# First block of a two-layer linear-attention kernel: values first, weight folding in pieces, one written order on all engines

## The chip, the core and the metric

The program runs on one core of one Trainium2 chip. A core has five engines with a queue each: TensorE (PE; matrix products, with PEld for its loads of the stationary operand), VectorE (DVE), ScalarE (ACT), GpSimd (POOL) and SyncE (SP, which here only issues DMA transfers). They run side by side and wait for each other by semaphores. The metric is device time in microseconds of one execution, lower is better. The median of three runs before the change is 1398.45 us (1397.73 to 1398.7).

## The reference

Two layers, each an attention part and a dense part, on x of 2048 rows by 640, all float32:

```
x = x + A(layernorm(x));  x = x + B(layernorm(x));  and both once more
A: q, k, v = x @ wqkv, 32 heads of 20
   pq = q @ w_phi[h], pk = k @ w_phi[h]
   phi = [softmax(p), softmax(-p)]            (40 features a head)
   o = phi_q (phi_k^T v) / (phi_q (phi_k^T 1) + 1e-6);  A = o @ wo
B: mish(x @ w1 + b1) @ w2, inner width 1536
```

The sums over all 2048 rows in phi_k^T v stand between the making of the features and their use, so A has a first pass over all rows (features of q and k, values, the sums) and a second one (averages, product with wo, residual).

## The kernel before, in words

Rows are taken in 8 blocks of 256, a block as two tiles of 128. Every float32 product with a weight is made of three faster ones: operand and weight are split into a high part (rounded by ACT, a copy) and a low part (DVE or POOL subtracts the high part from the original), and hi by hi, hi by lo and lo by hi are summed. A tile of 128 rows by 640 columns takes 2 halves of 320 columns x 5 chunks of the contraction x 3 = 30 products (`project`, `project_half`, line 344).

Since w_phi is linear, it is folded into the weights of q and k once, at the start: `fold_phi` (line 237) multiplies the transposed raw weights with a block-diagonal matrix `bd` of w_phi, piece by piece (5 chunks x 2 groups of columns). A product of it appears as two records of PE. A piece has three such products; ACT copies its high part out of PSUM and DVE makes the low part.

A block of x is normalised (`norm_stats` on DVE, `norm_scale` on POOL and DVE, `normed` on ACT), transposed on PE in three steps (`Transposed.step`, 4, 4 and 2 transposes, line 280) and split into hi and lo there (ACT copy line 116, DVE subtract line 286).

`attend_first` is the first pass. For each block and each tile it makes "k", "q" and "v" in an order given in a tuple; block 0 has v0, q0, v1, k0, q1, k1. Each of them is a Python generator: its products and the copy of the result out of PSUM come first, and each later step of the list advances the pending ones by one stage (row maxima and minima with the subtractions; exp on ACT; sums, reciprocal on DVE and the scaling on POOL; for q the transpose on DVE, line 425, and four transfers to DRAM, line 429; for k the sums over rows on PE, line 416).

PSUM holds two wide tiles ("mm", for the result of a project) and four narrow ones ("one", for folding, transposes and the sums). A q result goes to one of two buffers (`query_tile`), which is free again when the four transfers of the q tile two before it have landed. `v_tile` has two buffers, `row_tile` ("xn") four, `big_tile` five, `x_tile` two.

What sets the order: the whole is traced in one block that a planner orders, engine by engine, by a model of the times. Within `tc.manual_schedule(engines=...)` the instructions of the engines named keep the order in which they were written; other instructions can still be placed between them. Before the change only SP is written by hand at the start: transfers of `bd` and the raw q weights, of block 0 of x, the rest of them, then the value weights `wv`, then the raw k weights. `tc.issue_after(ins)` keeps what is traced on that instruction's engine behind it; `act()` uses it to chain ACT's instructions. Folding of the q weights stands before the first products, folding of the k weights before k0.

Of the kernel before, what the change touches and what calls it, by code (L numbers as in the profile page):

```python
# [8 lines left out]
F32 = mybir.dt.float32  # L9
# [7 lines left out]
P = 128  # L17
S = 2048
D = 640
# [23 lines left out]
def kernel(  # L43
# [63 lines left out]

    last_act = [None]

    def act(*args, **kw):  # L110

        if last_act[0] is None:
            ins = nc.scalar.activation(*args, **kw)
        else:
            with tc.issue_after(last_act[0]):
                ins = nc.scalar.activation(*args, **kw)
        last_act[0] = ins.ins
# [4 lines left out]

    def split(hi, lo, src, stage):

        st = stage()[:, :D]
        nc.sync.dma_start(st, src)
        nc.scalar.activation(hi, st, AF.Copy)
        nc.vector.tensor_tensor(lo, st, hi.bitcast(F32), op=ALU.subtract)
# [37 lines left out]

    def load_v_weights():

        ws = [r1_pair(k) for k in range(KD)]
        for k in range(KD):  # L170
            split(ws[k][0][:, D:2 * D], ws[k][1][:, D:2 * D], wv[k * P:(k + 1) * P, :],
                  (row_tile, row_tile, v_tile, v_tile, big_tile)[k])
        return ws

# [52 lines left out]
    def fold_phi(ws, bd, raw):  # L227

        pss = {}
        for k, c in ((0, 0), (1, 0), (2, 0), (3, 0), (0, 1), (1, 1), (2, 1), (3, 1), (4, 0), (4, 1)):  # L230
            if c == 0:
                mm = None if k % 2 else mm_tile()
                pss[k] = [one_tile(), one_tile()] if k % 2 else [mm[:, 0], mm[:, 1]]
            ps = pss[k][c]
            for t in range(3 * c, 3 * c + 3):
                r, rows = raw[t]
                nc.tensor.matmul(ps[:, (t % 3) * 120:(t % 3) * 120 + rows],
                                 r[:rows, k * P:(k + 1) * P], bd[:rows, t, :rows],
                                 start=True, stop=True)
            n0, n1 = (0, 360) if c == 0 else (360, D)  # L240
            hi, lo = ws[k][0][:, n0:n1], ws[k][1][:, n0:n1]
            nc.scalar.activation(hi, ps[:, :n1 - n0], AF.Copy)
            nc.vector.tensor_tensor(lo, ps[:, :n1 - n0], hi.bitcast(F32), op=ALU.subtract)

# [83 lines left out]

    def project(xts, t, ws, col, ps=None):

        if ps is None:
            mm = mm_tile()
            ps = [mm[:, 0], mm[:, 1], mm]
        for c in range(2):
            project_half(ps[c], xts, t, ws, col, c)
        return ps
# [10 lines left out]
    def both(ps):  # L347

        return ps[2][:, :, :HC]


    def query_tile(i):
        return r2_wide(10 + i % 2, F32).rearrange("p s d -> p (s d)")

    def features(ps, e, pool_sub):
# [11 lines left out]
        for s, op in ((0, ALU.max), (1, ALU.min)):  # L367
            nc.vector.tensor_reduce(m[:, s], eh[:, 1], axis=AX.X, op=op)
        (nc.gpsimd if pool_sub else nc.vector).tensor_tensor(
            eh[:, 0], eh[:, 1], m[:, 0].unsqueeze(2).to_broadcast([P, H, DH]), op=ALU.subtract)  # L370
        nc.vector.tensor_tensor(eh[:, 1], m[:, 1].unsqueeze(2).to_broadcast([P, H, DH]), eh[:, 1],
                                op=ALU.subtract)
        yield
# [13 lines left out]
    def attend_first(layer, x_src, first):  # L387


        def fetch_normed(b):  # L390
            if layer:
                return load_turned(n2_d[b], [row_tile] * 3)
            xt = fetch(x_src, b)
            norm_scale(b, [norm_stats(t, xt) for t in range(BT)])
            return xt
# [24 lines left out]

        def queries(xts, i, ps=None):
            e = query_tile(i)
            yield from features(project(xts, i % BT, q_ws, 0) if ps is None else ps, e, True)

# [7 lines left out]

        def values(xts, i, v):
            vv = v.rearrange("p (h d) -> p h d", d=DH + 1)
            act(vv[:, :, DH], ident[:, :H], AF.Copy, scale=0.0, bias=1.0)
            if i < BT:
                pv = project(xts, i, kv_ws, D, [one_tile(), one_tile()])
                for c in range(2):
                    act(vv[:, c * H // 2:(c + 1) * H // 2, :DH],
                        pv[c][:, :HC].rearrange("p (h d) -> p h d", d=DH), AF.Copy)  # L440
            else:
                pv = project(xts, i % BT, kv_ws, D)
                act(vv[:, :, :DH].rearrange("p (c h) d -> p c h d", c=2),
                    both(pv).rearrange("p c (h d) -> p c h d", d=DH), AF.Copy)
            yield

        if first is None:
            with tc.manual_schedule(engines={mybir.EngineType.SP}):
                bd = big_tile()[:120, :720].rearrange("p (t c) -> p t c", t=6)
                nc.sync.dma_start(bd[:, :3], phi_bd[:, :3])  # L450
                raw = load_raw(0, range(3))
                xt = fetch_normed(0)
                nc.sync.dma_start(bd[:, 3:], phi_bd[:, 3:])
                raw += load_raw(0, range(3, 6))
                nxt = normed(0, xt).all()
                q_ws = [r2_pair(k) for k in range(KD)]
                fold_phi(q_ws, bd, raw)
                kv_ws = load_v_weights()
                raw = load_raw(1)
            nc.sync.dma_start(mask, head_mask)  # L460
        else:
            nxt, kv_ws = first
            q_ws = load_q_weights()
        for b in range(NB):
            xts = nxt
            order = ("k0", "k1", "v0", "v1", "q0", "q1")
            if b == 0:
                order = ("v0", "q0", "v1", "k0", "q1", "k1")
            elif b == 1:
                order = ("k0", "q0", "k1", "v0", "q1", "v1")  # L470
            elif b == NB - 1:
                order = ("k0", "k1", "v0", "v1", "q0")
            vs = [v_tile() for _ in range(BT)]
            for n, (kind, t) in enumerate(order):
# [5 lines left out]
                if b == 0 and n == 3:  # L480
                    if layer == 0:
                        fold_phi(kv_ws, bd, raw)
                    kva, kvz = one_tile(), one_tile()
                if b == NB - 1 and n == 3:
                    loaded = {0: load(0)}
                if b + 1 < NB:
                    if n == 0:
                        xt = fetch_normed(b + 1)
                    elif n == 2:
# [3 lines left out]
                g = {"k": lambda: keys(xts, i, vs[t]), "q": lambda: queries(xts, i),  # L493
                     "v": lambda: values(xts, i, vs[t])}[kind]()
                next(g)
                advance()
                pending.append(g)
            if b == 1:
                if layer == 0:
                    spill_qk_weights(kv_ws, q_ws)  # L500
                o_ws = load_o_weights()

        def rest():
# [8 lines left out]
            project_half(ps[1], xts, 1, q_ws, 0, 1, range(3, KD))  # L512
            pending.append(queries(xts, NT - 1, ps))
            next(pending[-1])
# [166 lines left out]
    def dense(x_src, x_dst, w1s, w2s, first, last):  # L681
# [97 lines left out]
        for i in range(len(steps) + SKEW):  # L779
# [26 lines left out]
            if i == len(steps) - 1 and not last:  # L806
                with tc.issue_after(exps[0]):
                    kv_ws = load_v_weights()
            if i >= SKEW:
# [89 lines left out]
```

## Time and profile before

| what | value |
|---|---|
| median of three runs | 1398.45 us |
| the profiled execution's own time | 1396.09 us |
| its span, first to last instruction | 1394.3 us |
| PE busy | 1380.7 us (99%) |
| DVE, ACT, POOL busy | 1075.5, 583.3, 440.0 us |
| DMA, q1, share of 16 engines | 44.2% |
| granted TensorE clock, mean | 0.999 |

The profiled execution is 2.36 us below the median of the runs, and its span 1.79 us below its own time. In a timeline a row gives start, duration, engine, line and operation, `x4` that four instructions in a row are merged into it (it then ends with the last one's end), and in brackets the engine's idle time before it with what ended it. Products overlap in PE's pipe, so the cost of one is the distance between two starts and not its duration. In the rows `mm<-big,raw` and `one<-big,raw` are folding, `one<-ident,xn` transposes, and products with `r1` use the value and k weights, those with `r2` the q weights.

### The profile page before, as it was taken

To read this page: it belongs to the slowest core of one execution; us is meant where nothing else is said; L and a number is where in the kernel's file an instruction comes from. 1 tells how busy PE (TensorE), PEld (TensorE's weight loads), DVE (VectorE), ACT (ScalarE), POOL (GpSimd) and SP (SyncE) were. 2 spreads that over 40 slices of the span, in tenths; PEclk is the share of its full clock that TensorE was granted. 3 is DMA by queue.
4 is the path that set the end of the run, shared out by engine and by line. 5 is a ranking of instruction groups with operands and counts; after the bars stand their busy time and mean duration, and the time that the engine had idled before them with its cause. 6 is when DMAs were issued, how large, how long until landed. Compare 5 with 4: busy or idle time off the path is not lost. (4 is left out here: it accounts for less than half of the span.)

```text
span 1394.3 us, 28137 instructions
## 1 busy us (share of the span) xinstructions
PE 1380.7 (99%) x11528; PEld 1367.0 (98%) x11528; DVE 1075.5 (77%) x1820; ACT 583.3 (42%) x973; POOL 440.0 (32%) x334
## 2 busy tenths in 40 slices
PE   7999999999999999999999999999999999999998
PEld 7999999999999999999999999999999999999998
DVE  5797877796698877788769988888767876777775
ACT  4444433321355454545454333332235444444443
POOL 1353443343422221222234434343342211211112
PEclk9999999999999999999999999999999999999999
DMA  8533333689633432343474333357976212333200
GB/s 328 162 79 54 67 52 58 184 228 307 235 86 95 114 84 62 83 114 95 122 261 87 71 57 58 65 107 231 288 257 200 76 25 72 95 95 95 75 22 20
DMA packets 350035, 169.57 MB, mean 122 GB/s; under 512 B 286866, under 2 KB 323458, under 8 KB 349906
## 3 DMA queue, kind: packets, MB, share of 16 engines
q1 hardware_dynamic: 349906, 167.78, 44.2%
q8 instruction: 90, 1.47, 0.4%
q14 instruction: 39, 0.32, 0.1%
HBM read 104.82 MB, written 62.91 MB: 120 GB/s over the span
## 5 line engine op out<-in xcount | busy, mean ns | idle before, releaser
L737 PE MATMUL mm<-r2h,ol 128*128 128x320 f32 x1280 | 304.7, 309 | 0.0
L721 POOL TENSOR_TENSOR ol<-big,ol 128x512 fp32r<-128x512 f32 (+1 forms) x98 | 129.8, 1324 | 483.5 <-ACT ol L720 407.3
L695 PE MATMUL one<-xtl,r1h 128*128 128x256 f32 x960 | 268.2, 279 | 0.0
L695 PE MATMUL one<-xth,r1l 128*128 128x256 f32 x960 | 268.0, 279 | 0.0
L695 PE MATMUL one<-xth,r1h 128*128 128x256 f32 x960 | 265.9, 279 | 0.0
L737 PEld LDWEIGHTS mm<-r2h,ol 128*128 128x128 f32 x1280 | 219.1, 188 | 0.0
L737 PE MATMUL mm<-r2l,ol 128*128 128x320 f32 x640 | 197.3, 309 | 0.0
L344 PE MATMUL mm<-r1h,xth 128*128 128x320 f32 x600 | 187.3, 312 | 0.0
L344 PE MATMUL mm<-r1h,xtl 128*128 128x320 f32 x600 | 186.0, 310 | 0.7 <-DVE xtl L286 0.7
L344 PE MATMUL mm<-r1l,xth 128*128 128x320 f32 x600 | 186.0, 310 | 0.0
L695 PEld LDWEIGHTS one<-xtl,r1h 128*128 128x128 f32 x960 | 180.4, 188 | 0.0
L695 PEld LDWEIGHTS one<-xth,r1l 128*128 128x128 f32 x960 | 180.4, 188 | 0.0
L695 PEld LDWEIGHTS one<-xth,r1h 128*128 128x128 f32 x960 | 179.6, 188 | 0.0
L710 DVE TENSOR_SCALAR big<-big 128x512 f32<-128x512 f32 (+1 forms) x98 | 57.1, 583 | 109.9 <-ACT big L708 109.7
L379 POOL TENSOR_TENSOR r<-r,r 128x1280 f32<-128x1280 f32 x32 | 75.8, 2368 | 163.1 <-DVE r L378 157.3
L737 PEld LDWEIGHTS mm<-r2l,ol 128*128 128x128 f32 x640 | 120.2, 188 | 0.0
L712 ACT ACTIVATE big<-big,two 128x512 f32<-128x512 f32 (+1 forms) x98 | 70.1, 715 | 116.2 <-DVE big L711 116.1
L708 ACT ACTIVATE big<-one,b1s 128x256 f32<-128x256 f32 x192 | 80.8, 467 | 90.1 <-PE one L695 89.6
L720 ACT ACTIVATE ol<-big 128x512 fp32r<-128x512 f32 (+1 forms) x98 | 61.0, 622 | 136.0 <-DVE big L719 135.9
L344 PEld LDWEIGHTS mm<-r1h,xth 128*128 128x128 f32 x600 | 112.8, 188 | 1.3
L344 PEld LDWEIGHTS mm<-r1h,xtl 128*128 128x128 f32 x600 | 112.7, 188 | 1.3 <-DVE xtl L286 1.0
L344 PEld LDWEIGHTS mm<-r1l,xth 128*128 128x128 f32 x600 | 112.8, 188 | 0.1
(129 smaller groups left out, 3156.1 us busy)
## 6 DMA issues: line engine op xcount, KB each, us to landing
e_d<-r SPq DMA_DIRECT2D x128, 160.0 KB, 4.0
big<-e_d SPq DMA_DIRECT2D x32, 640.0 KB, 6.6
x_d<-xt SPq DMA_DIRECT2D x23, 640.0 KB, 3.9
xt<-x_d SPq DMA_DIRECT2D x22, 640.0 KB, 4.3
n_d<-xn SPq DMA_DIRECT2D x176, 80.0 KB, 2.1
xt<-in_x SPq DMA_DIRECT2D x16, 640.0 KB, 5.9
xn<-x_d SPq DMA_DIRECT2D x28, 320.0 KB, 4.2
v<-n_d SPq DMA_DIRECT2D x30, 256.0 KB, 3.3
```

Source lines behind the costliest of these rows:

```text
L344: nc.tensor.matmul(ps[:, :HC], a[:, sl], r, start=(k == 0 and n == 0), stop=(k == KD - 1 and n == 2))
L379: nc.gpsimd.tensor_tensor(eg, eg, r.unsqueeze(2).to_broadcast([P, 2 * H, DH]), op=ALU.mult)
L695: nc.tensor.matmul(ph[:, j, :], l, r, start=(n == 0), stop=(n == 3 * KD - 1))
L708: exps[0] = nc.scalar.activation(part(ta, 0)[:, j - js.start], ph[:, j, :], AF.Exp, bias=b1s[:, 2 * pr + j:2 * pr + j + 1]).ins
L710: nc.vector.tensor_scalar_min(e, e, E_CAP)
L712: nc.scalar.activation(r, n, AF.Ln, bias=two)
L720: nc.scalar.activation(ah[:, js], n, AF.Copy)
L721: nc.gpsimd.tensor_tensor(al[:, js], n, ah[:, js].bitcast(F32), op=ALU.subtract)
L737: nc.tensor.matmul(pys[t][:, c, :HC], l[:, j, sl], r, start=(f == 0 and n == 0), stop=(f == KF - 1 and n == 2))
```

## The change

- Ahead of everything PE makes 58 transposes of the identity into a PSUM tile that nobody reads.
- In the first layer the start and block 0 are written by hand on PE, SP, ACT, DVE and POOL (`written()`), and `act()` adds no chain there.
- Order of the transfers: block 0 of x, the five chunks of `wv`, `bd` in one, the raw q weights, the raw k weights, block 1 of x, block 2 of x, the mask.
- Block 0's second tile is normalised on DVE, the first on ACT. The splitting of `wv` chunk k stands between the transpose steps.
- The values of both tiles are made first, chunk by chunk, in the two wide PSUM tiles; behind chunks 0 to 4 stand 0, 2, 3, 3 and 2 pieces of the folding of the q weights. `fold_phi` becomes a generator that takes a narrow PSUM tile for each piece, the first column group of all chunks first.
- Block 0's order is v0, v1, q0, q1, k0, k1. The ten pieces of the folding of the k weights stand between the ten half-chunks of q0's products. Block 1's normalisation begins at q0.
- In the first layer, from block 1 on, the statistics of the next block are issued behind the last subtraction of the features on DVE; in both layers the making of the wo weights, after block 1, is issued on ACT behind its last chained instruction.

```
-        pss = {}
-        for k, c in ((0, 0), (1, 0), (2, 0), (3, 0), (0, 1), ...):
...
+        for c in range(2):
             n0, n1 = (0, 360) if c == 0 else (360, D)
+            for k in range(KD):
+                ps = one_tile()
...
+                nc.scalar.activation(hi, ps[:, :n1 - n0], AF.Copy)
+                nc.vector.tensor_tensor(lo, ps[:, :n1 - n0], hi.bitcast(F32), op=ALU.subtract)
+                yield
...
+    warm = one_tile()
+    for _ in range(58):
+        nc.tensor.transpose(warm[:, :P], ident, ident)
...
     def project(xts, t, ws, col, between=None, ps=None):
...
+            for k in range(KD):
+                project_half(ps[c], xts, t, ws, col, c, range(k, k + 1))
+                next(between, None)
...
-            with tc.manual_schedule(engines={mybir.EngineType.SP}):
-                bd = big_tile()[:120, :720].rearrange("p (t c) -> p t c", t=6)
...
+            writing.enter_context(written())
+            xt = fetch(x_src, 0)
+            mvs = [norm_stats(t, xt) for t in range(BT)]
...
+            make_v(0)
+            norm_scale(0, mvs)
+            xn = [row_tile() for _ in range(BT)]
+            act(xn[0], xt[:, 0, :], AF.Identity, ...)
+            nc.vector.tensor_scalar(xn[1], xt[:, 1, :], ...)
+            early[2] = fetch(x_src, 2)
...
+            for k, pieces in enumerate((0, 2, 3, 3, 2)):
+                for t in range(BT):
+                    for c in range(2):
+                        project_half(v01[t][c], nxt, t, kv_ws, D, c, range(k, k + 1))
+                for _ in range(pieces):
+                    next(fold)
...
-                order = ("v0", "q0", "v1", "k0", "q1", "k1")
+                order = ("v0", "q0", "v1", "k0", "q1", "k1") if layer else ("v0", "v1", "q0", "q1", "k0", "k1")
...
+                        with nullcontext() if start or layer else tc.issue_after(last_sub[0]):
+                            xt = fetch_normed(b + 1)
...
+            if start:
+                writing.close()
...
-                o_ws = load_o_weights()
+                with tc.issue_after(last_act[0]):
+                    o_ws = load_o_weights()
```

More of the change, by code (lines that the diff above doesn't have):

```diff
@@ L1 @@
-from contextlib import ExitStack
+from contextlib import ExitStack, contextmanager, nullcontext
 import concourse.bass as bass
@@ L349, in both @@
         return ps[2][:, :, :HC]
+    last_sub = [None]
     def query_tile(i):
@@ L445, in values @@
             yield
-        if first is None:
-            with tc.manual_schedule(engines={mybir.EngineType.SP}):
-                bd = big_tile()[:120, :720].rearrange("p (t c) -> p t c", t=6)
[L450 to L459, printed above, removed]
-            nc.sync.dma_start(mask, head_mask)
+        @contextmanager
@@ L473, in attend_first @@
             vs = [v_tile() for _ in range(BT)]
+            start = b == 0 and not layer
             for n, (kind, t) in enumerate(order):
@@ L479, in attend_first @@
                         load_k_weights(kv_ws)
-                if b == 0 and n == 3:
-                    if layer == 0:
-                        fold_phi(kv_ws, bd, raw)
+                if b == 0 and n == 4:
                     kva, kvz = one_tile(), one_tile()
@@ L492, in attend_first @@
                         nxt.step()
-                g = {"k": lambda: keys(xts, i, vs[t]), "q": lambda: queries(xts, i),
-                     "v": lambda: values(xts, i, vs[t])}[kind]()
+                g = {"k": lambda: keys(xts, i, vs[t]), "q": lambda: queries(xts, i, fold_phi(kv_ws, bd, raw_k) if start and n == 2 else None),
+                     "v": lambda: values(xts, i, vs[t], v01[t] if start else None)}[kind]()
                 next(g)
@@ L807, in dense @@
                 with tc.issue_after(exps[0]):
-                    kv_ws = load_v_weights()
+                    kv_ws = [r1_pair(k) for k in range(KD)]
+                    for _ in load_v_weights(kv_ws):
+                        pass
             if i >= SKEW:
```

107 lines of the change are left out of this document (69 added, 38 removed).

## The prediction

> **What bounds the kernel.** I read the page first, then the busy times by stretch, then PE's own order of time at the start. The page says that PE is busy for all but 13.6 us and that the chain that ended last is nearly all PE. The stretches are cut at the first product (17.31) and at the first product of k1 (52.47); columns are length, then busy us of each engine.
>
> ```profile
> span 1394.3 us, 28137 instructions
> PE 1380.7 (99%) x11528; PEld 1367.0 (98%) x11528; DVE 1075.5 (77%) x1820; ACT 583.3 (42%) x973; POOL 440.0 (32%) x334
> PE 44%; DVE 0%; issue 0%; DVEq 0%
> ...
> 0.00:17.31 17.31, 10.19 (x46) 9.39 (x47) 7.10 (x23) 7.23 (x13) 3.21 (x12) 1.00 0.90 317
> 17.31:52.47 35.16, 35.16 (x248) 33.65 (x246) 21.30 (x48) 17.32 (x36) 6.68 (x10) 1.00 0.78 292
> 260.00:1394.30 1134.30, 1127.87 (x9633) 1119.33 (x9631) 875.26 (x1528) 474.72 (x809) 335.22 (x257) 1.00 0.44 123
> ```
>
> So PE sets the time everywhere, 7.1 us of its 13.6 idle us lie ahead of 17.31, and 6.4 behind 260, which the change does not touch. What a change of block 0 can win is what PE loses at the start, idle or slow. Its order of time there:
>
> ```profile
> 4.12 1.18 PE L237 MATMUL mm<-big,raw 120*128 120x120 f32 x4 [4.12 <-DMA raw<-in_wqk_t]
> 5.84 2.07 PE L237 MATMUL mm<-big,raw 120*128 120x120 f32 x8 [0.55 <-DMA raw<-in_wqk_t]
> 10.37 2.04 PE L237 MATMUL mm<-big,raw 120*128 120x120 f32 x8 [2.46 <-DMA raw<-in_wqk_t]
> 12.33 1.07 PE L237 MATMUL mm<-big,r 40*128 40x40 f32 x4
> 13.34 0.90 PE L280 MATMUL one<-ident,xn 128*128 128x128 f32 x3
> 14.03 1.47 PE L237 MATMUL one<-big,raw 120*128 120x120 f32 x6
> 15.29 1.59 PE L280 MATMUL one<-ident,xn 128*128 128x128 f32 x7
> 16.72 0.83 PE L237 MATMUL mm<-big,raw 120*128 120x120 f32 x6
> 17.31 0.39 PE L344 MATMUL mm<-r2h,xth 128*128 128x320 f32 x1
> ...
> 24.79 0.42 PE L344 MATMUL one<-r1h,xth 128*128 128x320 f32 x1
> 25.04 0.31 PE L344 MATMUL one<-r1l,xth 128*128 128x320 f32 x1
> ...
> 36.42 1.28 PE L237 MATMUL one<-big,raw 120*128 120x120 f32 x10
> 37.63 0.41 PE L237 MATMUL one<-big,r 40*128 40x40 f32 x2
> 37.98 0.70 PE L237 MATMUL one<-big,raw 120*128 120x120 f32 x4
> ...
> 39.93 0.66 PE L280 MATMUL one<-ident,xn 128*128 128x128 f32 x4
> 40.43 0.60 PE L237 MATMUL mm<-big,raw 120*128 120x120 f32 x4
> ...
> 48.07 0.31 PE L344 MATMUL mm<-r2h,xth 128*128 128x320 f32 x1
> 52.47 0.31 PE L344 MATMUL mm<-r1h,xth 128*128 128x320 f32 x1
> ```
>
> From start to start a folding record costs (37.63 - 36.42)/10 = 0.121 us late and (15.29 - 14.03)/6 = 0.21 early; a transpose (40.43 - 39.93)/4 = 0.125 late and (16.72 - 15.29)/7 = 0.204 early. So the clock is about half until some 16.6, 6.3 us after PE's work from 10.37 on became unbroken; the burst from 4.12 to 7.9, 3.8 us, did not open it. A small folding record costs (37.98 - 37.63)/2 = 0.175, a product (52.47 - 48.07)/30 = 0.147, and the first product behind a fold 25.04 - 24.79 = 0.25, that is 0.1 more.
>
> At 17.31 PE has done 32 folding records, 4 small ones and 10 transposes: 3.9 + 0.7 + 1.25 = 5.8 us at late prices. It has lost 17.31 - 5.8 = **11.5 us**. At 52.47 it has done 150 products, 100 + 20 folding records and 20 transposes: 22.0 + 12.1 + 3.5 + 2.5 = 40.1, so it has lost 12.4. All that follows is a comparison with that number, for the same work.
>
> **The start.** The changed PE begins with 58 transposes as soon as the identity is there, and its first real work is a transpose of x.
>
> ```profile
> 0.99 0.29 POOL masks.py:199 TENSOR_SCALAR_AFFINE_SELECT ident<-ident 128x128 f32<-128x128 f32 x1
> 8.91 1.66 DVE L250 BATCH_NORM_STATS2 bn<-xt 128x6 f32<-128x320 f32 x4
> 12.25 0.92 ACT L113 ACTIVATE xn<-xt,stats 128x640 f32<-128x640 f32 x1 [3.83 <-DVE stats L262]
> 40.63 0.60 ACT L116 ACTIVATE xth<-one 128x512 fp32r<-128x512 f32 x1 [0.19 <-PE one L280]
> 41.26 0.69 DVE L286 TENSOR_TENSOR xtl<-one,xth 128x512 fp32r<-128x512 f32 x1 [0.22 <-ACT xth L116]
> 2.00:4.00 2.00, 0.00 (x0) 0.00 (x0) 0.00 (x0) 0.00 (x0) 0.00 (x0) 1.00 0.87 269
> ```
>
> The 58 start at about 1.4. If the clock opens 3.9 us later, 19 of them are slow and they end at 1.4 + 3.9 + 39 x 0.125 = 10.2; at 0.11 a transpose (the folds from 16.72 to 17.31 show 0.098), 9.6; if 6.3 us later, 30 are slow and they end at 11.2. I take 10.2. Two transfers of 489 KB together released PE at 4.12; x of block 0, 655 KB, now goes first, so at 269 GB/s and a little more it lands at about 4.7. From statistics to the normalised tile took 12.25 + 0.92 - 8.91 = 4.3 us, hence 9.0: the warming, not x, sets the first transpose. From there (39.93) to the first low part (41.26 + 0.69) are 2.0 us, in which PE does 10 transposes and 2 products (1.55 us). Lost: 10.2 + 2.0 - 1.55 = 10.7, which is **-0.8**; the ends are 10.1 and 11.7. [...] The weights are no wait: a wv chunk, 0.33 MB, lands every 1.2 us, from 5.9 on, and chunk k is wanted 1.8 us apart from 12 on; bd and the first half of the q weights, 3.0 MB behind x, are there by about 14 at the 317 GB/s of the first stretch, and wanted at 15.6. Splitting wv (ACT and DVE) is covered by the 12 products of a chunk; without that cover it would cost PE its 0.8 us a chunk.
>
> **Folding between products.** Same records; but before, some 6 groups of products begin behind a fold, afterwards 3 among the values and 10 in q0: 7 more at 0.1, **+0.7** (0 to 1.0).
>
> **v0's copy.** Both wide tiles hold values until ACT has copied them, and q0 needs v0's. ACT's written order has the last two pieces' high parts first, so the copy comes only when PE has nothing left that it may do.
>
> ```profile
> 19.64 0.29 ACT L116 ACTIVATE v<-ident 128x32 f32<-128x32 f32 x1
> ...
> 45.57 0.40 ACT L242 ACTIVATE r1h<-mm 128x280 fp32r<-128x280 f32 x1 [2.23 <-PE mm L237]
> ...
> 61.47 0.71 ACT L116 ACTIVATE big<-mm 128x640 f32<-128x640 f32 x1 [1.84 <-PE mm L344]
> ```
>
> 0.40 + 0.29 + 0.71 end to end, of which the small copies overlap a little, and 0.1 to get PE going: **+1.4** (1.1 to 1.8). No work covers this.
>
> **The narrow tiles.** Block 1's statistics begin when q0 does, and its two normalisations stand on ACT ahead of the k pieces' high parts. Statistics to the end of one normalisation took 4.3 us, with a second 0.92 it is 5.2; PE meanwhile fills four narrow tiles, 5 x 0.44 + 4 x 0.75 = 5.2 us. With the copy and subtraction of the first piece (0.9) and the late start of q0: **+0.3** (0 to 1.2). The statistics moved to DVE's queue here hold nothing but fold low parts.
>
> **The q buffers.** Here the reordering shows later. q2's copy needs q0's transfers landed; v2's products need q2's wide tile.
>
> ```profile
> 48.27 0.71 ACT L116 ACTIVATE big<-mm 128x640 f32<-128x640 f32 x1 [2.29 <-PE mm L344]
> 48.87 1.26 ACT L116 ACTIVATE r<-r 128x1280 f32<-128x1280 f32 x1
> ...
> 58.06 1.51 DVE L425 STREAM_TRANSPOSE r<-r 128x1280 f32<-128x1280 f32 x1 [0.75 <-POOL r L379]
> 59.49 1.50 DVE L368 TENSOR_REDUCE m<-big 128x32 f32<-128x640 f32 x2
> ...
> 66.20 0.70 ACT L116 ACTIVATE r<-mm 128x640 f32<-128x640 f32 x1 [2.86 <-DMA e_d<-r]
> ...
> 70.07 0.31 PE L344 MATMUL mm<-r1h,xth 128*128 128x320 f32 x1
> ```
>
> k0's copy at 48.27 releases q0's exp; q0's transpose ends at 59.57 and q2's copy, which waited for the transfers, at 66.90: 18.6 us after k0's copy. v2 starts at 70.07, five groups of 30 products (22.0) after it: 3.2 to spare. In the new order only k1, k2, q2 and k3 stand between: 17.6 us. If q0's chain takes as long, PE waits **+1.0**. Other PE work (transposes, sums of k0) may fill it: 0. The upper end is the first rival. -0.2 for the small stalls that stood among the early folds.
>
> **Nothing elsewhere.** The spills and wo loads go on SP behind landed data; wo's high parts move behind block 1 on ACT (42% busy), where they hold no product. DVE pays 0.7 for the second tile's normalisation, under the wait for ACT's. If ACT's slack were gone, the five wo copies of some 0.7 would cost 3.5.
>
> **Sum.** -0.8 + 0.7 + 1.4 + 0.3 + 1.0 - 0.2 = +2.4 us. The profiled execution's 1396.09 (span 1394.3) would become 1398.5; the median lies 2.36 higher, so 1400.8. About 0.2%, 2.8 us, is what a measurement here tells from nothing: the forecast is no change that can be told, close to the edge.
>
> **Rivals.**
>
> Slower: DVE takes block 2's statistics and k1's reductions before q0's transpose. They used to be done early; now they are held behind k0's subtraction and become ready just where q0's chain needs DVE. Price: 1.66 + 0.3 and 1.50 on top of the 1.0: +3.4, 1404.3; with k1's subtractions 1.6 more. It speaks for it that DVE is idle for 13.9 of the 35.2 us before 52.47 and that work moved out of there meets a full queue; against it, that DVE took that transpose at once at 58.06. It decides from 0.4 us of delay on, the sum being 2.4.
>
> The warming doesn't do what it says. Then 58 x 0.204 = 11.8 end at 13.2, the first transposes and some 5 us of products run at half clock: 3 + 0.8 + 2.5 more, 1407.1. Against it: in the 3.4 us before the clock opened, 10 of 16 records were transposes. [...] The rows 13.34 to 16.72 speak against it.
>
> Faster: x alone sets the first transpose (9.0, lost 9.5) and neither v0's copy nor a buffer holds PE; 12.4 - 9.5 gives -2.9, 1395.5. It decides only if v0's copy hides wholly, and ACT's order speaks against that.
>
> **How the numbers follow.** Forecast case 0.57 (own range 1399.0, with the low ends of start, narrow tiles and q buffers, to 1401.9), of which 0.07 lies over the 2.8; DVE rival 0.31, cold clock 0.07, faster 0.05. Faster 0.05, same 0.50, slower 0.31 + 0.07 + 0.07 = 0.45. The range leaves out the cold clock and half of the faster case: 1396 to 1406, the top with k1's subtractions.
>
> **What would show it.** The first product at 11.5 to 12.7; transposes at 0.11 to 0.125 from start to start by then; PE idle 1.2 to 1.8 before q0's first product, released by ACT's copy of v; a short idle at the fifth k piece; PE idle 1 to 5 at v2 while ACT waits for transfers of q0. If PE has no gap after q0's first product, the sum is 1.3 too high and more; if the 58 end after 12 or q0's transpose comes 3 us later than its scaling on POOL, the time is 1404 or above.

## The result and the profile after

The changed kernel takes 1409.26 us (median of four, 1408.5 to 1410.46) beside 1398.3 us for the kernel before: a ratio of 1.0079, 95% interval 1.0062 to 1.0097, or 11.0 us more. The forecast was 1400.8 with a range up to 1406; the time lies outside it. The profiled execution took 1409.36 us, near its median, while that of the kernel before stood 2.36 us below its own. Differences of the two profiles are therefore up to 2.4 us larger than those of the medians.

From the page of the changed kernel:

```profile
span 1407.6 us, 28237 instructions
PE 1387.7 (99%) x11586; PEld 1373.0 (98%) x11586; DVE 1081.8 (77%) x1821; ACT 582.9 (41%) x970; POOL 443.7 (32%) x334
```

PE is idle for 1407.6 - 1387.7 = 19.9 us in place of 13.6. The table by stretch says where (start and end, length, then busy us of PE, PEld, DVE, ACT, POOL, the granted clock, DMA share, GB/s):

```profile
0.00:17.31 17.31, 15.51 (x109) 14.79 (x110) 8.82 (x21) 7.76 (x12) 2.25 (x9) 1.00 0.91 304
17.31:60.00 42.69, 40.90 (x286) 38.94 (x285) 21.53 (x41) 16.81 (x33) 3.63 (x5) 1.00 0.67 246
60.00:100.00 40.00, 31.77 (x244) 30.59 (x242) 36.28 (x49) 13.76 (x20) 19.50 (x12) 0.87 0.34 64
```

One stretch stands out, and it lies behind the rewritten block: from 60 to 100 us PE is idle for 8.2 us, and the clock is 0.87. The waits of PE, each line with the total, the number and the longest:

```profile
PE mm L350 <- ACT r L120: 8.2, 1, 8.2
...
PE one L424 <- POOL big L387: 1.3, 1, 1.3
PE mm L350 <- ACT v L117: 1.2, 1, 1.2
```

The 8.2 us are one wait, of v2's first product for the copy of q2 out of the wide tile. PE's order of time around the places of the forecast:

```profile
1.34 8.25 PE L90 MATMUL one<-ident 128*128 128x128 f32 x58 [1.34 <-POOL ident masks.py:199]
9.82 1.31 PE L281 MATMUL one<-ident,xn 128*128 128x128 f32 x10 [0.24 <-ACT xn L117]
11.17 0.41 PE L350 MATMUL mm<-r1h,xth 128*128 128x320 f32 x1
...
11.91 0.42 PE L350 MATMUL mm<-r1h,xtl 128*128 128x320 f32 x1 [0.19 <-DVE xtl L287]
...
29.95 0.42 PE L350 MATMUL mm<-r2h,xth 128*128 128x320 f32 x1 [1.21 <-ACT v L117]
...
35.69 0.93 PE L238 MATMUL one<-big,raw 120*128 120x120 f32 x6 [0.58 <-DVE r1l L243]
...
53.33 0.40 PE L350 MATMUL mm<-r1h,xth 128*128 128x320 f32 x1
...
79.40 0.63 PE L350 MATMUL mm<-r1h,xth 128*128 128x320 f32 x1 [8.23 <-ACT r L120]
79.83 0.47 PE L350 MATMUL mm<-r1l,xth 128*128 128x320 f32 x1
80.10 0.47 PE L350 MATMUL mm<-r1h,xtl 128*128 128x320 f32 x1
```

The start went as forecast. k1 begins at 53.33 in place of 52.47, so up to the end of block 0 the change costs **0.9 us**. Then come the **8.2 us** idle. And behind it products start 0.267 us apart (twelve steps from 79.83 to 83.03) where 0.147 is usual: the clock had fallen to half in the idle time. 15 products lie in the slow stretch, 15 x (0.267 - 0.147) = **1.8 us**. A cut of that stretch shows the clock, 0.51 in it:

```profile
73.00:83.40 10.40, 4.00 (x15) 4.00 (x16) 6.90 (x11) 4.75 (x6) 3.63 (x2) 0.51 0.95 153
```

0.9 + 8.2 + 1.8 = 10.9 us, against 11.0 between the medians. The profiles agree with that in the first layer: the first product of the dense part starts at 386.5 in place of 375.4, 11.1 us later. Their spans differ by 13.3 us, so some 2.2 us more come in the second layer, among them a wait of 1.3 us for POOL at L424 where the profile before has 0.3. Since the profiled execution of the kernel before lies 2.36 us below its median, the medians do not settle how much of those 2.2 us is the change.

Why was q2's copy so late? It writes into the buffer that q0's transfers must have left. ACT's, DVE's and POOL's rows of that chain in the changed kernel:

```profile
53.39 0.70 ACT L117 ACTIVATE big<-mm 128x640 f32<-128x640 f32 x1 [3.64 <-PE mm L350]
...
78.65 0.70 ACT L120 ACTIVATE r<-mm 128x640 f32<-128x640 f32 x1 [14.37 <-DMA e_d<-r]
```

```profile
55.56 0.42 DVE L287 TENSOR_TENSOR xtl<-one,xth 128x256 fp32r<-128x256 f32 x1 [2.09 <-ACT xth L117]
...
58.95 1.48 DVE L385 TENSOR_REDUCE r<-r 128x64 f32<-128x1280 f32 x1
60.34 1.66 DVE L251 BATCH_NORM_STATS2 bn<-xt 128x6 f32<-128x320 f32 x4
61.92 1.53 DVE L376 TENSOR_REDUCE m<-big 128x32 f32<-128x640 f32 x2
63.37 1.47 DVE L385 TENSOR_REDUCE r<-r 128x64 f32<-128x1280 f32 x1
64.76 0.54 DVE L386 RECIPROCAL r<-r 128x64 f32<-128x64 f32 x1
...
66.76 1.73 DVE L377 TENSOR_TENSOR big<-big,m 128x640 f32<-128x640 f32 x1
...
70.29 1.50 DVE L433 STREAM_TRANSPOSE r<-r 128x1280 f32<-128x1280 f32 x1
```

```profile
65.45 2.37 POOL L387 TENSOR_TENSOR r<-r,r 128x1280 f32<-128x1280 f32 x1 [12.84 <-DVE mv L253]
```

ACT copies k0 and then makes q0's exp; q0's sums end on DVE at 60.43. Its reciprocal, half a microsecond of work, starts at 64.76: block 2's statistics, k1's reductions and q1's sums stand ahead of it on DVE. POOL's scaling ends at 67.82, and the transpose starts 2.5 us after it, behind subtractions of the k tiles. From k0's copy to the end of the transpose are 71.79 - 53.39 = 18.4 us, where before it was 59.57 - 48.27 = 11.3; from there to q2's copy 6.9, before 6.6. The whole chain took 26.0 us in place of 18.6, and PE's products between still took 17.6.

Nearly all of the 7.4 us that it grew by lies in three places. From k0's copy to the start of q0's sums it takes 5.6 us in place of 2.9 (58.95 - 53.39, 51.20 - 48.27), from there to the reciprocal 5.8 in place of 3.8 (55.03 - 51.20 before), and from the start of the scaling to the transpose 4.8 in place of 2.4 (58.06 - 55.65). In the first place DVE even stands idle for 2.1 us, up to 55.56: its written order has the low part of block 1's last transposes ahead of k0's reductions, and that low part waits for ACT, while k0's copy is there at 54.09. So a part of the growth is the written order and not the amount of work; ordered by the planner (below), the sums start 2.9 us behind k0's copy again (57.73 - 54.80).

DVE came out of block 0 behind. Busy times up to the end of k1's products, before the change and after it:

```profile
0.00:56.95 56.95, 49.83 (x321) 47.52 (x322) 32.88 (x76) 25.53 (x49) 13.15 (x23) 1.00 0.77 282
```

```profile
0.00:57.80 57.80, 54.21 (x378) 51.53 (x379) 28.18 (x59) 22.70 (x43) 5.88 (x14) 1.00 0.77 273
```

DVE is the third figure: 32.88 us done before, 28.18 after, 4.7 us less at the same point of PE's work. Those 4.7 us stand in DVE's queue in the stretch that follows, where it has little idle time (36.28 of 40 us busy from 60 to 100; in the kernel before 40.00 of 40).

### The profile page after: what moved, and what is told of

Read it like the earlier page. It is cut to its first block, busy times and chain, and to the rows that moved or that the text cites. A ratio compares the mean times of both kernels' runs of the same rounds, so it can differ in the third digit from the quotient of the medians.

```text
span 1407.6 us, 28237 instructions
## 1 busy us (share of the span) xinstructions
PE 1387.7 (99%) x11586; PEld 1373.0 (98%) x11586; DVE 1081.8 (77%) x1821; ACT 582.9 (41%) x970; POOL 443.7 (32%) x334
## 5 line engine op out<-in xcount | busy, mean ns | idle before, releaser
L350 PE MATMUL mm<-r1h,xth 128*128 128x320 f32 x620 | 195.2, 315 | 8.3 <-ACT r L120 8.2
L350 PE MATMUL mm<-r1h,xtl 128*128 128x320 f32 x620 | 192.5, 310 | 0.9 <-DVE xtl L287 0.9
L350 PE MATMUL mm<-r1l,xth 128*128 128x320 f32 x620 | 192.9, 311 | 0.0
L350 PEld LDWEIGHTS mm<-r1h,xth 128*128 128x128 f32 x620 | 117.2, 189 | 10.3 <-ACT r L120 8.5
L350 PEld LDWEIGHTS mm<-r1h,xtl 128*128 128x128 f32 x620 | 117.2, 189 | 1.4 <-DVE xtl L287 1.4
L350 PEld LDWEIGHTS mm<-r1l,xth 128*128 128x128 f32 x620 | 117.3, 189 | 0.1
```

The lines of the kernel that those rows point to most:

```text
L350: nc.tensor.matmul(ps[:, :HC], a[:, sl], r, start=(k == 0 and n == 0), stop=(k == KD - 1 and n == 2))
```

## The experiments

All edits are to the changed kernel, except in the one that adds a part to the kernel before. Ratios are to the kernel before, run again beside each (medians of 1398.15 to 1398.56), with a 95% interval.

**Is the q buffer the cost?** q2 of the first layer alone is written to another tile, so that nothing waits for q0's transfers.

```
-            e = query_tile(i)
+            e = big_tile() if i == 2 and not layer else query_tile(i)
```

> The changed kernel, with q2 alone written to one of the five big tiles, so that its copy does not wait for q0's transfers. Nothing else is moved. Theory (buffer wait): no idle before v2, 1399 to 1400. Rival (DVE behind as a whole): idle moves to q3 or k4, time above 1405.

1400.07 us, ratio 1.0012 (1.0003 to 1.0022): 9.2 us back. Its waits:

```profile
PE one L424 <- POOL big L387: 2.1, 2, 1.3
```

The 8.2 us and the fall of the clock behind them are gone (granted clock 1.00 from 60 to 100 us); the first sums over k wait 0.8 more for POOL. 8.2 + 1.8 - 0.8 = 9.2, the measured difference. That it fits to a tenth is in part luck, since the profiled execution also has something that the changed kernel's had not: behind the wait for v0's copy (1.2 us in both) products run at half pace, up to about 33.4 (rows in the last section), and k1 begins at 54.23 in place of 53.33. The buffer carries the loss, and what is left (1.8 us over the kernel before) is the rest of the change.

**Can the order of block 1 hide it?** Both k tiles of block 1 come first, then the first tile's values, and only then q2.

```
-                order = ("k0", "q0", "k1", "v0", "q1", "v1")
+                order = ("k0", "k1", "v0", "q0", "v1", "q1") if layer == 0 else ("k0", "q0", "k1", "v0", "q1", "v1")
```

> The changed kernel, with block 1 of the first layer made in the order k0, k1, v0, q0, v1, q1, so that q2 comes two groups of 30 products (8.8 us) later and its copy asks later for the buffer of q0. Theory (the 8.2 us of PE idle before v2, and the half clock behind it, come from q2's copy waiting for q0's transfers): the idle falls from 8.2 to under 1 us, the clock stays full, and the time falls by 8.2 + 1.8 us to 1399 to 1400. Rival (DVE as a whole is behind, whatever the order): an idle of 5 us or more appears at another copy and the time stays above 1405.

1407.52 us, 1.0064 (1.0049 to 1.0079). The wait moved:

```profile
PE one L424 <- POOL big L387: 6.9, 2, 5.7
```

v2 no longer waits, but the sums over k0's and k1's features now wait 5.7 us for POOL's scaling, which stands behind DVE's work, and again PE comes back slow: 22 records of those sums take 2.53 us at 82.00, where the kernel before has 1.38 at 71.48. The theory that one late buffer is all there is missed; the rival, that DVE as a whole is behind and the next thing that needs it waits, holds.

**Are block 2's statistics to blame?** The rule that holds them behind the last subtraction is dropped.

```
-                        with nullcontext() if start or layer else tc.issue_after(last_sub[0]):
+                        with nullcontext():
```

> The changed kernel without the rule that holds the statistics of the next block behind the last subtraction of the features. Block 2's statistics then stand among the folds, before q0's chain. Theory (DVE does other work ahead of q0's reciprocal and transpose: 6.8 us, of which the statistics are 1.9): the idle before v2 falls from 8.2 to about 6 us, the time to 1406 to 1408. My first rival of the prediction (statistics are most of it): idle 4 us or less, time 1403 or less.

1409.44 us, 1.008 (1.0065 to 1.0095), no change. DVE's rows of this kernel:

```profile
39.67 1.67 DVE L251 BATCH_NORM_STATS2 bn<-xt 128x6 f32<-128x320 f32 x4 [0.86 <-DMA xt<-in_x]
...
71.26 1.50 DVE L433 STREAM_TRANSPOSE r<-r 128x1280 f32<-128x1280 f32 x1
```

The statistics now run at 39.67, among the folds. In this execution k0's copy starts at 54.51, 1.1 us later than in the changed kernel, and the transpose comes 16.8 us behind it, where it came 16.9 behind it before that edit: other ready work takes the statistics' place. PE's wait is 8.0 us. Statistics alone are not the cause.

**Is it DVE's order?** The written order is drawn out into block 1's first step, with q0's and q1's sums, reciprocals and q0's transpose ahead of k1's reductions; the statistics of block 2 then come one step later.

```
-        def advance():
-            for g in pending[::-1]:
+        def advance(order=None):
+            for g in order or pending[::-1]:
...
-                    if n == (2 if start else 0):
+                    if n == (2 if start else 1 if b == 1 and not layer else 0):
...
-                advance()
+                first_k = b == 1 and n == 0 and not layer
+                advance([pending[j] for j in (1, 0, 2, 3)] if first_k else None)
...
-            if start:
+                if first_k:
-                writing.close()
+                    writing.close()
```

> The changed kernel, with the written order carried on through the first step of block 1, DVE there doing q0's reciprocal, q1's sums and reciprocal and q0's transpose ahead of k1's reductions, and block 2's statistics one step later. The buffers are as in the changed kernel. Theory (it is DVE's order that makes q0's chain 26.0 us long where 18.6 were taken before): q0's transpose ends near 65 instead of 71.8, the idle before v2 is 1 to 2 us, the clock stays full, 1399.5 to 1402. Rival (the place of q2, four groups behind k0's copy, is the cause, or the transfers are slow): idle 4 us or more and a time above 1404.

1410.26 us, 1.0083 (1.0068 to 1.0098). DVE's rows, and PE's longest wait:

```profile
64.91 1.51 DVE L433 STREAM_TRANSPOSE r<-r 128x1280 f32<-128x1280 f32 x1 [0.62 <-POOL r L387]
...
74.61 1.66 DVE L251 BATCH_NORM_STATS2 bn<-xt 128x6 f32<-128x320 f32 x4
```

```profile
PE one L281 <- ACT xn L120: 6.9, 1, 6.9
```

The transpose stands at 64.91 in place of 70.29. The whole chain, from k0's copy at 54.73 to the end of q2's at 73.84, takes 19.1 us, nearly the 18.6 of the kernel before, and the wait for q2 falls from 8.2 to 1.4 us, which is the size of the forecast. So it was DVE's order that made the chain long. But the time is the same: block 2's statistics, which this edit also puts a step later, now come at 74.61, and its first transposes wait 6.9 us for them. One loss was exchanged for another of the same size, as it would be if DVE's backlog was only put in another order; the next run tests that.

**And with the statistics done where DVE has room?** The same, with block 2's statistics written into block 0.

```
+                if start and n == 3:
+                    ahead2 = fetch_normed(2)
+                if b == 1 and n == 0 and not layer:
+                    xt = ahead2
```

> The kernel with DVE's written order carried into block 1 (q0's chain ahead of k1's reductions), and block 2's statistics written into block 0, before q1's products, where DVE stands idle. The buffers are as in the changed kernel. Theory (DVE came out of block 0 with 4.7 us less done than before, 28.2 against 32.9 us at the end of k1's products, and whichever work stands last in its order is late: q0's transpose in the changed kernel, block 2's statistics when q0 is put first): with the statistics done in idle time both are in time but for 1 to 1.5 us at v2, the clock stays full, 1400 to 1401.5. Rival (DVE is short by more than the statistics): an idle of 4 us or more of PE at some third place, 1403 or more.

1400.47 us, 1.0016 (1.0007 to 1.0025), with the q buffers as in the change. PE waits 1.3 us for q2, and the granted clock from 60 to 100 us is 1.00.

Work moved back into DVE's idle time of block 0 and the order together win what the buffer wins. Neither alone did (the two runs above, of which the second also made the statistics later). This is the forecast's own case: q2 waits 1.3 us, where 1.0 was predicted.

**Is it the writing by hand?** Only SP stays written; the other engines are ordered by the planner, and ACT's chain is back.

```
-            in_written[0] = True
+            in_written[0] = False
-            with tc.manual_schedule(engines={... "PE", "SP", "Activation", "DVE", "Pool"}):
+            with tc.manual_schedule(engines={mybir.EngineType.SP}):
```

> The changed kernel with SP alone written by hand as before, PE, ACT, DVE and POOL ordered by the planner, the order v0, v1, q0, q1, k0, k1 kept. Theory (the order of the tiles leaves DVE with too little to do early and makes q0 late; writing the other engines by hand is not the cause): PE still waits 5 us or more at q2's copy and the time is 1405 or more. Rival (the hand-written order of block 0 makes DVE late): wait under 2 us, 1401 or less.

1405.63 us, 1.0043 (1.0027 to 1.0058). The wait for q2 is still there, 3.7 us in place of 8.2, and the granted clock is 0.91 from 40 to 60 us and 0.89 from 60 to 90. So the new order of tiles (q0's chain with only four tiles behind it) makes PE wait in either case, and the written order makes that wait 4.5 us longer. Half of either theory. What the written order costs in all is less sure than the medians' 3.6 us: the four executions lie between 1402.97 and 1406.66, and in the profiled one products also run at half pace, 0.27 us apart, from 44.7 to 47.6, behind 3.8 us of folding and with no wait of PE just before them. Why the clock fell there is not shown.

**What is the warming worth?** The 58 transposes alone, added to the kernel before:

```
+    warm = one_tile()
+    for _ in range(58):
+        nc.tensor.transpose(warm[:, :P], ident, ident)
```

> The kernel before with nothing but the 58 transposes ahead. They end near 9.6 with the clock open; the folds that ran at half clock from 4.1 to 12.3 start there instead, and the 10 transposes and 6 folds up to 16.7 run at 0.11 to 0.12 instead of 0.21. Theory (warming alone is worth what the slow records from 12.3 to 16.6 cost, 16 x 0.09 us and the small folds): the first product at 15.5 to 16, 1 to 1.8 us less, 1396.8 to 1397.6. Rival (the start of the kernel before is bound by its transfers and x, so the time saved is waited for again): within 0.5 us of the kernel before.

1403.31 us, 1.0037 (1.0024 to 1.0051): slower by 5 us, not faster. Its PE and DVE rows say why:

```profile
10.14 1.50 PE L240 MATMUL mm<-big,raw 120*128 120x120 f32 x12
...
17.16 0.90 PE L283 MATMUL one<-ident,xn 128*128 128x128 f32 x3 [2.69 <-ACT xn L116]
...
21.76 0.61 PE L347 MATMUL mm<-r2h,xth 128*128 128x320 f32 x1
```

```profile
12.85 1.66 DVE L253 BATCH_NORM_STATS2 bn<-xt 128x6 f32<-128x320 f32 x4
```

In the old order the first folding is ready at 4.12; behind the warming it starts at 10.14. On DVE its low parts stand ahead of the statistics of x, which come at 12.85 in place of 8.91, so the first transpose comes at 17.16 in place of 13.34. PE waits 2.7 us for it, and the clock that the warming had opened is lost again: from 17.1 to 23.8 it is 0.53, and the seven transposes from 19.13 to 20.62 cost 0.21 us each, as in the kernel before. The first product comes at 21.76 in place of 17.31, 4.5 us later. The work behind the warming got the delay and none of the speed, except for the first folds (12 records in 1.50 us, 0.125 each).

The other way round, the change with q2 in another tile (as above), without the 58:

```
-    warm = one_tile()
-    for _ in range(58):
-        nc.tensor.transpose(warm[:, :P], ident, ident)
```

> The kernel with q2 in a big tile (1400.1 us), without the 58 transposes of the identity. If they open the clock ahead of the work: transposes of x and the products of the first chunks run at half clock, 10 x 0.1 + 0.45 x 3 to 6 us, so 2 to 3.7 us slower, 1402 to 1403.8, and the clock's record starts near 13 to 16 instead of 4.9. If they bring nothing here: within 0.5 us of 1400.1.

1402.35 us, 1.0028 (1.0017 to 1.0039), 2.3 us slower than with them.

```profile
9.96 2.40 PE L278 MATMUL one<-ident,xn 128*128 128x128 f32 x10 [9.96 <-ACT xn L114]
12.01 0.62 PE L347 MATMUL mm<-r1h,xth 128*128 128x320 f32 x1
12.43 0.47 PE L347 MATMUL mm<-r1l,xth 128*128 128x320 f32 x1
...
14.83 0.32 PE L347 MATMUL mm<-r1l,xth 128*128 128x320 f32 x1
```

Here PE has nothing to do before 9.96 anyway; the warming lies in time that is free, and its absence costs a late first product (12.01 for 11.38 with them) and ten slow products, nine steps of 0.267 from 12.43 to 14.83. The price of the same 58 transposes is -2.3 us in one order and +5 us in the other.

**v0's copy.** With q2 in another tile, v0 is copied between the last two pieces of folding, and block 1's statistics stand ahead of the last chunk.

```
+            g01 = [values(None, t, vs[t], v01[t]) for t in range(BT)]
...
+                if k == 4:
+                    ahead1 = fetch_normed(1)
...
+                    if k == 4:
+                        next(g01[t])
+                        next(fold)
-                for _ in range(pieces):
+                for _ in range(pieces if k < 4 else 0):
```

> The kernel with q2 in a big tile, and v0's copy written between the last two folding pieces (chunk 4 of tile 0, copy of v0, a piece, chunk 4 of tile 1, copy of v1, a piece), block 1's statistics before chunk 4. Theory (the 1.2 us before q0 come from ACT's written order, the 0.6 us at the fifth k piece from statistics begun only with q0): both go, 1.8 us less, 1398 to 1398.6. Rival (q0 waits there for something else): no change, 1400.

1398.12 us, 1.0002 (0.9993 to 1.0011): 1.95 us better than with the buffer alone. Its waits no longer show v (1.2), and with that wait the slow products behind it are gone too: in the two profiles k1 begins at 51.23 in place of 54.23. The fifth piece's 0.6, the other part of the theory, stands in the changed kernel's profile and not in that of the kernel with q2 in another tile, so the theory's 1.8 us came out partly for another reason. The longest wait left is that for POOL at L424, 2.1 us in two parts: 0.8 in the first layer and 1.3 in the second.

With DVE's order and the early statistics of the runs above added to it:

> Both: v0's copy and block 1's statistics early, q2 in a big tile, DVE's order with q0's chain first and block 2's statistics in block 0. Theory: PE idles less than 1 us between its first product and 260, and the time is that of the kernel before or up to 1.5 us below it, 1397 to 1398.3.

1398.16 us, 1.0 (0.9991 to 1.0009). The two mends for q0's chain do not add: the 0.8 us that PE waited at L424 in the first layer are gone, but a wait of 0.9 us for a copy by ACT is new.

**The waits that are left, at L424.** First, in the kernel with v0's copy early, the rule that holds the wo copies on ACT is kept in the first layer only:

```
-                with tc.issue_after(last_act[0]):
+                with nullcontext() if layer else tc.issue_after(last_act[0]):
```

> The kernel with q2 in a big tile and v0's copy early (1398.1 us), with the rule that holds the making of the wo weights behind ACT's last chained instruction kept in the first layer only. Theory (in the second layer this rule pushes POOL's low parts of wo into block 2, ahead of a k tile's scaling, for which PE's sums then wait 1.3 us): that wait is gone, 1396.8. Rival (the wait belongs to something else in the second layer): the wait stays, 1398.1.

1398.66 us, 1.0 (0.9992 to 1.0009); L424 still waits 2.6 us for POOL. The forecast time missed, but the theory had the cause of the wait. These are POOL's rows in the second layer of the changed kernel, where PE's sums at 796.06 wait 1.3 us:

```profile
787.87 5.23 POOL L150 TENSOR_TENSOR r2l<-raw,r2h 128x640 fp32r<-128x640 f32 x3
793.06 2.94 POOL L387 TENSOR_TENSOR big<-big,r 128x1280 f32<-128x1280 f32 x1
```

Three low parts of wo stand ahead of the scaling of a k tile. With the rule dropped in that layer they do not, and the sums at that place (783.96) no longer wait. In their stead the sums before them, at 772.07, wait 1.8 us for POOL; why, is not shown. The same edit with all the mends:

> The kernel with DVE's order, early statistics, early copy of v0 and q2 in a big tile (1398.2 us), with the wo rule in the first layer only. The 1.3 us of the second layer go: 1396.8, and 1.0 to 2.0 us under the kernel before.

1399.16 us, 1.0008 (0.9999 to 1.0017): the time missed too, with a wait of 1.7 us at 771.91. And with the rule dropped in both layers:

> As the kernel before this one, with the wo rule dropped in the first layer too, so that ACT makes some wo high parts among the folds of block 0 and POOL their low parts in its idle time. Theory (the same push stands behind the 0.8 us that PE waits for POOL in block 2 of the first layer): 0.5 to 1 us less, 1396 to 1396.3. Rival (the copies delay folds and PSUM copies on ACT in block 0): 1397 or more, with an idle of PE before 60 us.

1406.03 us, 1.0056 (1.0043 to 1.0069):

```profile
PE one L424 <- POOL big L387: 7.0, 2, 5.4
```

This theory missed as well: in the first layer the rule is needed. Without it the low part of a wo chunk stands ahead of k0's scaling on POOL. POOL is idle for 5.2 us, up to 81.39, until ACT has made the high part (at 80.57, when the chunk has landed), though DVE starts k0's reciprocal at 78.31; the scaling starts at 82.88, and the first sums over k wait 5.4 us in place of 0.8. Last, those sums are made one step later, in the kernel with v0's copy early and in the one with all mends:

```
-            if i % BT == 0 and BT < i < NT - BT:
+            if i % BT == 0 and BT <= i < NT - BT:
```

> The kernel with q2 in a big tile and v0's copy early (1398.1 us), with the sums of tile 2 on PE one step later, as those of tiles 4 to 12 are. Theory (what is left over the best sum is PE waiting for POOL's scaling of a k tile, 0.8 us in block 1 of the first layer and 1.3 us in the second): both waits under 0.3, 1396 to 1396.8. Rival (POOL is late as DVE is, the wait moves to the next sums): within 0.5 us of 1398.1.

> The same on the kernel with DVE's order and early statistics (1398.2 us). Theory: 1396 to 1397. Rival: within 0.5 us of 1398.2.

1399.39 us, 1.001 (1.0001 to 1.0018), and 1399.08 us, 1.0003 (0.9994 to 1.0012). In both the wait at L424 in the second layer falls from 1.3 to 0.3 us (in the former the 0.8 of the first layer stays), and in both a wait for the low part of the transposed x (`xtl`, made on DVE), in the second layer too, grows from 0.7 to 1.5. The rival had it right that the wait moves; the times are even 1.3 and 0.9 us above those of the two kernels they were made from. No version beat the kernel before by more than can be told.

## Why the prediction was wrong

By its own terms, in us:

| step | forecast | measured | shown by |
|---|---|---|---|
| start | -0.8 | -1.1 | lost 11.91 - 1.25 - 0.29 = 10.4 for 11.5 |
| v0's copy | +1.4 | +1.2 | wait at 29.95 |
| narrow tiles | +0.3 | +0.6 | wait at 35.69 |
| folding, small stalls | +0.5 | +0.2 | rest of the 0.9 at 53.33 |
| q buffers | +1.0 | +8.2 idle, +1.8 slow | wait at 79.40, pace behind it |
| sum | +2.4 | +10.9 | |

- **The start held.** The 58 ended at 9.6, the first transposes began at 9.82 (forecast 10.2) and the first product at 11.17 (a little before the 11.5 to 12.7 named). Ten transposes took 11.17 - 9.82 = 1.35, or 0.135 each; in the version without the warming they took 12.01 - 9.96 = 2.05. The rival of a cold clock is out. The 3.9 us after which the clock was to open, from which the -0.8 is worked out, were an estimate that no run shows: with the warming the pace changed 3.5 us after PE's first transpose (rows in the last section), without it after 14.83 - 9.96 = 4.9.
- **v0's copy, the narrow tiles and the folding held** to 0.3 us each. With the buffer's wait taken out the time was 1400.07, and the forecast without its q term is 1400.8 - 1.0 = 1399.8. That these agree to 0.3 us is in part luck: the 0.8 us more at L424 and the slow products behind v0's copy were in no term.
- **The step that failed** is the term of the q buffers: "If q0's chain takes as long, PE waits +1.0". The mechanism was named rightly (q2's copy waits for q0's transfers, v2 for q2's wide tile) and so was the time of the products between, 17.6. But the chain did not take as long: 26.0 us in place of 18.6. The length was read from a trace in which DVE entered block 1 with its work done, and carried over to one in which 4.7 us of that work are still to do and DVE's order puts them ahead of q0. With q0 first on DVE the chain took 19.1 us; with the statistics in idle time as well, the time was 1400.47, near the forecast.
- **The first rival had the place and some third of the price.** It put block 2's statistics and k1's reductions ahead of q0's transpose, for 3.4 us more than the forecast; the buffer's terms came out 8.2 + 1.8 - 1.0 = 9.0 above it. Those two did stand there, ahead of the reciprocal already; q1's sums and more subtractions stood there as well, and the chain grew by 7.4. Taking out the statistics alone moved nothing. "DVE took that transpose at once at 58.06", the argument against it, was a row of the kernel before, where DVE had less to catch up. The sign for 1404 and above, a transpose 3 us later than its scaling, was set too high: it came 2.5 us later, and most of the delay lay ahead of the scaling.
- **What no term had** is the price of an idle time itself: the clock fell to 0.51 in the 8.2 us, and half speed behind them cost 1.8 us more.
- **"Nothing elsewhere" left out a wait of some 1 us in the second layer**, 1.3 us at L424 in place of 0.3. The prediction asked only what wo's high parts hold on ACT, "where they hold no product"; POOL's low parts come behind them, and three of these stand ahead of a scaling that PE's sums need. Taking the rule or the early sums away removed this wait and put another in its place, so no run shows how to win it.

## What to carry to other kernels

When work is moved out of a stage where an engine is idle, add up what that engine has done by a fixed point of the bottleneck's work, before and after. The difference is a backlog, and it falls on whatever chain next needs that engine: reading the length of that chain from the old trace is not enough, and reordering the backlog alone only passed the wait on here (1407.5 and 1410.3 us), until some of it went back into idle time (1400.5). A wait of PE can cost more than its length: here 8.2 us cost 10.0, with the slow products behind it. And see what filler work for the clock puts off: the 58 transposes won 2.3 us where PE had nothing else to do, and cost 5 where they put off the folds and PE waited another 2.7 us behind them.

## What was not expected of the hardware

In the changed kernel the clock fell within the wait of PE, and the price came after it. PE stood idle from 71.2 to 79.4; the granted clock was 1.00 from 71.2 to 73.0 and 0.51 from 73.0 to 83.4, and the first 4 us of products ran at 0.267 us in place of 0.147. After 5.4 to 6.9 us of idle (wo copies free, block 1's order, q first) PE was slow too: the granted clock from 60 to 100 us was 0.91 in each, and in the last two 22 records of the sums took 2.53 us, where the kernel before has 1.38. With q first, products behind 1.39 us of idle started 0.147 apart. These rows are of the kernel with q first, on both sides of its two waits:

```profile
73.90 0.42 PE L350 MATMUL mm<-r1h,xth 128*128 128x320 f32 x1 [1.39 <-ACT r L120]
74.15 0.31 PE L350 MATMUL mm<-r1l,xth 128*128 128x320 f32 x1
74.30 0.31 PE L350 MATMUL mm<-r1h,xtl 128*128 128x320 f32 x1
...
85.89 2.53 PE L424 MATMUL one<-big,v 128*64 128x120 f32 x22
```

But a short wait was not always free. Behind the 1.21 us for v0's copy the changed kernel kept its pace (products at 30.20 and 30.35). In the kernel with q2 in another tile, whose work up to there is the same, the clock was 0.50 from 30.2 to 33.4 behind the same wait, and products started 0.27 apart:

```profile
30.14 0.64 PE L350 MATMUL mm<-r2h,xth 128*128 128x320 f32 x1 [1.21 <-ACT v L117]
30.57 0.47 PE L350 MATMUL mm<-r2l,xth 128*128 128x320 f32 x1
30.84 0.47 PE L350 MATMUL mm<-r2h,xtl 128*128 128x320 f32 x1
```

ACT's copy of k1, which waits for PE's products, starts 0.9 us later in that version than in the changed kernel (58.91 for 58.01), and 1.1 and 1.3 us later in two more (statistics free 59.13, q first 59.35), as such a stretch would make it. With block 1's order it starts at 58.35, and with q first and early statistics the first low part of the k weights is made at 35.07, as in the changed kernel (35.10). What decides it is not shown; ahead of that wait stand 1.9 us of folding (26.82 to 28.74 in the changed kernel), and in the version ordered by the planner the products 0.27 apart, from 44.7 on, came behind folding alone.

And transposes of a constant were enough to open it here. The 58 alone, in the changed kernel, cut where their pace changes:

```profile
1.34:4.86 3.52, 3.52 (x17) 3.52 (x18) 1.00 0.84 296
4.86:9.60 4.74, 4.73 (x43) 4.49 (x41) 1.00 1.01 330
```

A transpose that overlaps the cut counts in both rows. Before 4.86 one takes 3.52 / 17 = 0.21 us, from there on 4.74 / 43 = 0.11 us. The column of the granted clock says 1.00 in both rows: the trace's first record of the clock is at 4.8, and ahead of it the pace of equal instructions has to be read in its place. The same column is 0.51 in the stretch after the long wait, where the pace agrees with it.
